# Attention beside channel mix on one core: attention steps spread over two chunks, early batches placed by load arrival, token mix as scale and add

## The chip, the cores and the metric

One core of a Trainium2 chip. The time is the device time of one execution in microseconds (us); a kernel is quoted by the median of its runs. TensorE (PE) does matmuls and transposes, VectorE (DVE), ScalarE (ACT) and GpSimd (POOL) the rest; here GpSimd mostly issues loads. "Span" is the length of one profiled execution; the timed run is 1.7 to 1.9 us longer than its span. The "granted clock" is the share of TensorE's full clock that the profile says it was given: 1.00 is full speed.

## The reference, cut to what matters

```python
# B=8 batches, H=8 heads, S=576 tokens, D=64, M=32 memory slots; model width 512, hidden 1024
a   = softmax(phi over tokens)                 # [b, h, s, m]
k_m = einsum('bhsm,bhsd->bhmd', a, k)          # v_m the same from v
x   = softmax(q @ k_m.T / 8 over m) @ v_m      # heads side by side: [B, S, 512]

x_prev = x shifted by one token (zero ahead of the first)
xk = mu_k * x + (1 - mu_k) * x_prev            # token mix for the keys
xr = mu_r * x + (1 - mu_r) * x_prev            # token mix for the gate
out = sigmoid(xr @ w_r) * (relu(xk @ w_k)**2 @ w_v)
```

The channel mix (the last line) of batch b needs the attention of batch b. The kernel writes the mix as `(x - x_prev) * (mu - 1) + x`.

## The kernel before

The channel mix runs in nine chunks of 512 tokens. A chunk has 16 slots: 8 key steps, then gates and values. After the channel-mix step of a slot the program emits the attention steps that a plan puts there. In these traces VectorE, TensorE and ScalarE run their own instructions in the order in which the program emits them (in the kernel before, TensorE stops 4.0 us for the q of batch 2 with matmuls of chunk 0 behind it). So the plan decides both what fills TensorE's time and what stands in front of what.

```python
        return [                                      # plan of a batch: (slot relative to its chunk, step)
            (-12, exp_phi),
            (-11, tr_q(0)), (-11, tr_q(1)), (-11, tr_q(2)), (-11, tr_q(3))] + kvsteps + [
            (-5, scores(0, 0)), (-4, scores(0, 1)), (-3, scores(1, 0)), (-3, scores(1, 1)),
            (-1, zsum)] + late + [
            (1, spread(0, 0)), (1, spread(0, 1)), (2, spread(1, 0)), (2, spread(1, 1)),
            (3, values(0, 0)), ...                    # cut: two values in each of slots 3 to 6
            (7, diff(0)), (8, diff(1)),
            (9, mix(0, 0)), ...                       # cut: eight mixes, to slot 14
        ]

        def mix(d4, which):
            def go():
                dst = (xk_T, xr_T)[which]
                nc.vector.scalar_tensor_tensor(
                    dst[:, d4, b * S:(b + 1) * S], in0=st["d"][:, d4, :],
                    scalar=mu1[:, which * ND + d4:which * ND + d4 + 1], in1=st["x"][:, d4, :],
                    op0=AL.mult, op1=AL.add)
            return go
```

`kvsteps` are the sums over k and v (into `kvps`, `zps`), their norm and the transpose of k (`ktps`, copied to `kmT`). PSUM, the memory in which the matmuls of this kernel leave their results, is split here into three rings of buffers that are used again and again: keys use two (`pk`), gates and values share three (`tag="pv"`), and every attention step shares three more:

```python
    kvps = psum.tile([128, 2, 2, 2 * D], F32, name="kvps", tag="at", bufs=3)   # and zps, ktps, qtps,
    ps   = psum.tile([128, SEG], F32, name="zcps", tag="at", bufs=3)           # scps, rbps, nops
    pv   = psum.tile([128, Dm], F32, name="pv", tag="pv", bufs=3)              # and pr of the gates
```

A step that asks for a fourth "at" buffer waits until one of the three has been read out by VectorE or ScalarE.

The softmax here doesn't subtract the row's maximum and nothing guards it: scores larger than these inputs give would overflow.

## Time and profile before

| | before |
|---|---|
| median at the start (3 runs) | 287.25 us (284.94 to 287.82) |
| span of the profiled run | 284.2 us |
| TensorE busy | 223.9 us |
| VectorE busy | 170.0 us |
| first key matmul | 33.3 us |
| chunks 0 and 1 | 48.2 and 32.9 us |
| chunks 2 to 5 together | 111.1 us |
| chunks 6, 7, 8 | 19.2, 17.1, 17.4 us |

A chunk is counted from its first key matmul to that of the next (the last to its last matmul). The prediction shows the lines.

### The profile page before, as it was taken

The page shows a single profiled execution, that of the slowest core. Times are in us where ns is not written, and L with a number is a line of the kernel's source. Part 1 is how long each engine was busy: PE and PEld are TensorE (multiplying, and loading weights), DVE is VectorE, ACT ScalarE, POOL GpSimd, SP SyncE. Part 2 cuts the span into 40 slices and gives each one's busy share as a digit, 9 for nine tenths or more (in the row PEclk, how much of TensorE's full clock was granted, in tenths as well). Part 3 has the DMA queues.
Part 4 walks back from the last instruction along what each step waited for, and adds up shares of the span by engine and source line. Part 5 has one row for each costly group of instructions (what it writes and reads, how often), then busy time and mean ns, then how long its engine had stood idle before and what let it go on. Part 6 is the DMA issues. An engine that isn't in the chain of part 4 may idle for free. (4 is left out here: it accounts for less than half of the span.)

```text
span 284.2 us, 4445 instructions
## 1 busy us (share of the span) xinstructions
PE 223.9 (79%) x1711; PEld 118.0 (42%) x1737; DVE 170.0 (60%) x403; ACT 105.2 (37%) x221; POOL 43.0 (15%) x60
## 2 busy tenths in 40 slices
PE   0357594698667779877987799779987999999992
PEld 0235133354323445444544454445453554444441
DVE  7325663154587487739763976497668759733411
ACT  3002351422422732462247225722661373451730
POOL 8326241143300240024002400000000000000000
PEclk9999997999956999999999999999999999999998
DMA  7999999998980399339924993012101311402124
GB/s 141 202 204 202 201 191 201 204 195 163 182 102 0 84 128 193 81 87 124 197 76 89 118 201 77 0 39 74 38 2 38 86 27 37 111 2 112 37 45 103
DMA packets 59397, 31.22 MB, mean 110 GB/s; under 512 B 18408, under 2 KB 54768, under 8 KB 59376
## 3 DMA queue, kind: packets, MB, share of 16 engines
q0 software_dynamic: 41312, 16.78, 49.2%
q1 hardware_dynamic: 18064, 14.16, 19.6%
q8 instruction: 13, 0.21, 0.3%
q14 instruction: 8, 0.07, 0.1%
HBM read 38.28 MB, written 9.44 MB: 168 GB/s over the span
## 5 line engine op out<-in xcount | busy, mean ns | idle before, releaser
L389 PE MATMUL pk<-xkT,wk 128*128 128x512 bf16 x272 | 73.5, 401 | 7.7 <-DVE xkT L323 4.9
L394 ACT ACTIVATE rl<-pk 128x512 bf16<-128x512 f32 x72 | 42.9, 595 | 77.0 <-PE pk L389 77.0
L413 PE MATMUL pv<-wv,sq 128*128 128x512 bf16 x280 | 65.2, 379 | 1.2 <-issue 1.1
L395 DVE TENSOR_TENSOR sq<-rl 128x512 bf16<-128x512 bf16 x72 | 30.2, 425 | 44.6 <-ACT rl L394 44.3
L416 DVE SCALAR_TENSOR_TENSOR o<-th,pv 128x512 f32<-128x512 f32 x36 | 24.7, 687 | 35.3 <-PE pv L413 18.9
L389 PEld LDWEIGHTS <-wk 128*128 128x128 bf16 x288 | 27.8, 102 | 38.2 <-issue 16.0
L413 PEld LDWEIGHTS <-sq 128*128 128x128 bf16 x288 | 27.6, 98 | 30.6
L405 ACT ACTIVATE th<-pr 128x512 f32<-128x512 f32 x36 | 21.4, 596 | 44.2 <-PE pr L402 33.5
L402 PE MATMUL pr<-wr,xrT 128*128 128x512 bf16 x142 | 35.2, 379 | 0.1
L243 PE MATMUL qtps<-identity,q 128*64 128x128 bf16 x320 | 14.0, 242 | 15.7 <-ACT x L303 7.6
L261 ACT ACTIVATE e<-scps 128x288 bf16<-128x288 f32 x32 | 12.3, 410 | 35.8 <-PE scps L259 35.7
L303 ACT CAST x<-nops 128x288 bf16<-128x288 f32 x64 | 22.0, 405 | 9.1 <-PE nops L301 9.0
L323 DVE SCALAR_TENSOR_TENSOR xrT<-diff,mu,x 128x576 bf16<-128x576 bf16 x32 | 24.9, 810 | 0.0
L323 DVE SCALAR_TENSOR_TENSOR xkT<-diff,mu,x 128x576 bf16<-128x576 bf16 x32 | 24.5, 813 | 0.3
L402 PEld LDWEIGHTS <-xrT 128*128 128x128 bf16 x144 | 13.8, 98 | 14.5
L83 POOL DMA_DIRECT2D q<-in_q_dram x8 | 7.2, 898 | 81.3 <-PE qtps L243 78.8
L243 PEld LDWEIGHTS <-q 128*64 128x64 bf16 x320 | 11.5, 123 | 19.0 <-issue 10.4
L259 PE MATMUL scps<-qT,kmT 128*128 128x288 bf16 x64 | 12.7, 305 | 8.0 <-DVE kmT L234 7.8
L247 DVE COPY qT<-qtps 128x576 bf16<-128x576 bf16 x32 | 13.5, 452 | 7.9 <-PE qtps L243 7.4
L200 PE MATMUL kvps<-kv,em 128*64 128x256 bf16 (+1 forms) x200 | 14.4, 272 | 4.5 <-DMA kv<-in_v_dram 2.3
L301 PE MATMUL nops<-atn,vbd 128*128 128x288 bf16 x64 | 15.3, 308 | 1.2 <-DVE atn L292 0.8
L200 PEld LDWEIGHTS <-em 128*64 128x64 bf16 x360 | 12.8, 120 | 8.4 <-issue 8.4
(58 smaller groups left out, 166.3 us busy)
## 6 DMA issues: line engine op xcount, KB each, us to landing
out_dram<-o SPq DMA_DIRECT2D x40, 128.0 KB, 2.4
phm<-in_phi_dram SPq DMA_DIRECT2D x8, 512.0 KB, 6.6
q<-in_q_dram POOLq DMA_DIRECT2D x8, 512.0 KB, 8.1
kv<-in_k_dram POOLq DMA_DIRECT2D x8, 512.0 KB, 8.2
kv<-in_v_dram POOLq DMA_DIRECT2D x8, 512.0 KB, 9.9
out_dram<-o SPq DMA_DIRECT2D x16, 256.0 KB, 2.5
wk<-in_moe_w_k_dram POOLq DMA_DIRECT2D x4, 256.0 KB, 15.3
wv<-in_moe_w_v_dram POOLq DMA_DIRECT2D x1, 1024.0 KB, 15.7
```

The lines of the kernel that those rows point to most:

```text
L200: nc.tensor.matmul(o, lhsT=lhsT, rhs=rhs, start=first, stop=j == NB, skip_group_check=True)
L243: nc.tensor.matmul(ps[i * D:(i + 1) * D, j * 128:(j + 1) * 128], lhsT=q5[:, 2 * pr + i, j, :], rhs=identity, is_transpose=True, start=True ...
L301: nc.tensor.matmul(ps, lhsT=st["vbd"][:, pr // 2, pr % 2, :], rhs=st["at"][:, pr // 2, sl], start=True, stop=True)
L303: nc.scalar.copy(st["x"][:, pr, sl], ps)
L323: nc.vector.scalar_tensor_tensor(dst[:, d4, b * S:(b + 1) * S], in0=st["d"][:, d4, :], scalar=mu1[:, which * ND + d4:which * ND + d4 + 1], ...
L389: nc.tensor.matmul(pk, lhsT=wk_sb[:, di, fi * 128:(fi + 1) * 128], rhs=xk_T[:, di, t0:t0 + CT], start=(di == 0), stop=(di == ND - 1))
L394: nc.scalar.activation(rl, pk, AF.Relu, scale=0.5 ** 0.5)
L395: nc.vector.tensor_mul(st["sq"][:, fi, :], rl, rl)
L402: nc.tensor.matmul(pr, lhsT=xr_T[:, di, t0 + ts * 128:t0 + (ts + 1) * 128], rhs=wr_sb[:, di, :], start=(di == 0), stop=(di == ND - 1))
L405: nc.scalar.activation(th, pr, AF.Tanh, scale=0.5)
L413: nc.tensor.matmul(pv, lhsT=st["sq"][:, fi, ts * 128:(ts + 1) * 128], rhs=wv_sb[:, fi, :], start=(fi == 0), stop=(fi == NF - 1))
L416: nc.vector.scalar_tensor_tensor(o, in0=st["pr"][ts], scalar=1.0, in1=pv, op0=AL.add, op1=AL.mult)
```

## The change

The intent: (1) two free slots between dependent attention steps of a batch, so that TensorE does not stop for the step just ahead, over up to two chunks; (2) batches 0 and 1 placed where their loads arrive, batch 2 squeezed into chunk 1, and a batch's phi loaded just ahead of its k, q, v; (3) the mix as a scale (`tensor_scalar`) and an add, in place of one `scalar_tensor_tensor`. The diff cut to this:

```diff
-        def mix(d4, which):
-                nc.vector.scalar_tensor_tensor(dst..., in0=d, scalar=mu1..., in1=x, op0=AL.mult, op1=AL.add)
+        def mix(which, pr, n=1):
+                dst = (xk_T, xr_T)[which][:, pr:pr + n, b * S:(b + 1) * S]
+                t = work.tile([128, 2, S], BF16, name="mu_d", tag="mu_d")[:, :n]
+                for i in range(n):
+                    o = which * ND + pr + i
+                    nc.vector.tensor_scalar_mul(t[:, i], st["d"][:, pr + i, :], mu1[:, o:o + 1])
+                nc.vector.tensor_add(dst, st["x"][:, pr:pr + n], t)
...
+    def load_batch(b):
+        load_phi(b, nc.sync if b == 0 else nc.gpsimd)     # then k, q, v; reload() calls it for b + 2
...
+        if b <= 1:
+            at = [-1] * 5 if b == 0 else [9, 11, 12, 13, 14]      # batch 1: slots of chunk 0
...
+        plan = [
+            (-16, exp_phi),
+            (-14, tr_q(0)), (-14, tr_q(1)), (-13, tr_q(2)), (-13, tr_q(3)),
+            (-8, ekv(slice(0, 2))), (-8, norm_k), (-5, tr_k), (-5, norm_v), (-5, reload),
+            (-3, scores(0, 0)), (-3, scores(0, 1)), (-2, scores(1, 0)), (-2, scores(1, 1)),
+            (1, zsum),
+            (4, spread(0, 0)), (4, spread(0, 1)), (5, spread(1, 0)), (5, spread(1, 1)),
+            (6, values(0, 0)), ...                                # two values in each of slots 6 to 9
+            (10, diff(0, 2)), (11, mix(0, 0, 2)), (11, diff(2, 2)), (12, mix(0, 2, 2)),
+            (13, mix(1, 0, 2)), (14, mix(1, 2, 2)),
+        ]
+        first = {2: 0, 3: -8}.get(b, -16)          # batches 2 and 3 squeezed into fewer slots
+        return [(15 - (15 - r) * (15 - first) // 31, s) for r, s in plan]
```

Chunk 0 also does all its gates ahead of its values, and three buffer counts of work tiles change (`rl` 4 to 3, `th` 2 to 4, `diff` 2 to 1).

More of the change, by code (lines that the diff above doesn't have):

```diff
@@ L71, with load_phi @@
     loads = {}
-    def load_phi(b):
+    def load_phi(b, eng):
         phm = ld.tile([128, H, NB, M], F32, name="phm", tag="phm")
         pht = ld.tile([NT, H, M], F32, name="pht", tag="pht")
-        nc.sync.dma_start(
+        eng.dma_start(
             out=phm.rearrange("p h j m -> p h (j m)"),
             in_=phi[b, :, 0:TAIL, :].rearrange("h (p j) m -> p h (j m)", j=NB))
-        nc.sync.dma_start(out=pht, in_=phi[b, :, TAIL:S, :].rearrange("h s m -> s h m"))
+        eng.dma_start(out=pht, in_=phi[b, :, TAIL:S, :].rearrange("h s m -> s h m"))
         loads[b] = {"phm": phm, "pht": pht}
@@ L86, in load_rows @@
         nc.gpsimd.dma_start(out=dst[:NT, :, NB, :], in_=src[:, TAIL:S, :].rearrange("h s d -> s h d"))
-    def load_kv(b):
+    def load_batch(b):
+        load_phi(b, nc.sync if b == 0 else nc.gpsimd)
         load_rows(kvs[b % 2][:, 0], k[b])
+        load_rows(qs[b % 2], q[b])
         load_rows(kvs[b % 2][:, 1], v[b])
-    def load_q(b):
-        load_rows(qs[b % 2], q[b])
     for i in range(2):
@@ L99 @@
         nc.vector.memset(kmTs[i], 0.0)
-    load_phi(0)
-    load_q(0)
-    load_kv(0)
+    load_batch(0)
     mu2 = const.tile([2 * ND, 128], F32, name="mu2")
@@ L114 @@
     nc.gpsimd.dma_start(out=wv_sb, in_=moe_w_v.rearrange("(fo fi) d -> fi fo d", fi=128))
-    load_phi(1)
-    load_rows(kvs[1][:, 0], k[1])
-    load_q(1)
-    load_rows(kvs[1][:, 1], v[1])
+    load_batch(1)
     ident_f = const.tile([2 * ND, 2 * ND], F32, name="identf")
@@ L168, in attention, with ekv @@
         st = {}
-        L = loads[b]
         kv5, q5, em, kmT = kvs[b % 2], qs[b % 2], ems[b % 2], kmTs[b % 2]
         def exp_phi():
+            L = loads[b]
             nc.scalar.activation(em[:, 0:NB].rearrange("p j h m -> p h j m"), L["phm"], AF.Exp)
             nc.scalar.activation(em[:NT, NB], L["pht"], AF.Exp)
-            if b + 2 < B:
-                load_phi(b + 2)
-        def ekv(parts, with_z):
+        def ekv(parts):
             w = parts.stop - parts.start
+            with_z = parts.start == 0
             def go():
-                if "kvps" not in st:
-                    st["kvps"] = psum.tile([128, 2, 2, 2 * D], F32, name="kvps", tag="at", bufs=3)
+                kvps = psum.tile([128, 2, w, 2 * D], F32, name="kvps", tag="at", bufs=3)
+                for i in range(w):
+                    st["kv"[parts.start + i]] = kvps[:, :, i, :]
                 if with_z:
@@ L194, in go @@
                                     rhs = kv5[:, parts, 2 * pr:2 * pr + 2, j, :]
-                                    o = st["kvps"][jj * 64:(jj + 1) * 64, c, parts, :]
+                                    o = kvps[jj * 64:(jj + 1) * 64, c]
                                 else:
@@ L198, in go @@
                                     o = st["zps"][jj * 64:(jj + 1) * 64, c:c + 1]
-                                first = j == 0 and c == 0 and (what == 1 or parts.start == 0)
-                                nc.tensor.matmul(o, lhsT=lhsT, rhs=rhs, start=first,
+                                nc.tensor.matmul(o, lhsT=lhsT, rhs=rhs, start=j == 0 and c == 0,
                                                  stop=j == NB, skip_group_check=True)
-                if parts.stop == 2 and b + 2 < B:
-                    load_kv(b + 2)
             return go
@@ L211, in norm_k @@
                 nc.vector.scalar_tensor_tensor(
-                    kbd[:, c].rearrange("p h d -> p (h d)"), in0=st["kvps"][:, c, 0, :],
+                    kbd[:, c].rearrange("p h d -> p (h d)"), in0=st["k"][:, c, :],
                     scalar=rz[:, c:c + 1], in1=maskk.rearrange("p h d -> p (h d)"),
@@ L220, in norm_v @@
                 nc.vector.scalar_tensor_tensor(
-                    vbd[:, c], in0=st["kvps"][:, c, 1:2, :].to_broadcast([128, 2, 2 * D]),
+                    vbd[:, c], in0=st["v"][:, c].unsqueeze(1).to_broadcast([128, 2, 2 * D]),
                     scalar=st["rz"][:, c:c + 1], in1=maskv.rearrange("p j h d -> p j (h d)"),
@@ L224, in norm_v, with reload @@
             st["vbd"] = vbd
+        def reload():
+            if b + 2 < B:
+                load_batch(b + 2)
         def tr_k():
@@ L247, in go @@
                 nc.vector.tensor_copy(st["qT"][:, pr, :], ps[:, 0:S])
-                if pr == NPAIR - 1 and b + 2 < B:
-                    load_q(b + 2)
             return go
@@ L304, in values, with diff @@
             return go
-        def diff(part):
+        def diff(pr, n=1):
             def go():
-                x = st["x"]
-                if part == 0:
-                    st["d"] = work.tile([128, ND, S], BF16, name="diff", tag="diff")
-                d = st["d"]
-                if part == 0:
-                    nc.vector.tensor_sub(d[:, :, 128:TAIL], x[:, :, 128:TAIL], x[:, :, 0:TAIL - 128])
-                else:
-                    nc.vector.tensor_sub(d[:, :, 1:128], x[:, :, 1:128], x[:, :, TAIL - 128:TAIL - 1])
-                    nc.vector.tensor_copy(d[:, :, 0:1], x[:, :, 0:1])
-                    nc.vector.tensor_sub(d[:, :, TAIL:S], x[:, :, TAIL:S], x[:, :, TAIL - 1:S - 1])
+                if "d" not in st:
+                    st["d"] = work.tile([128, ND, S], BF16, name="diff", tag="diff", bufs=1)
+                x, d = st["x"][:, pr:pr + n], st["d"][:, pr:pr + n]
+                nc.vector.tensor_sub(d[:, :, 128:TAIL], x[:, :, 128:TAIL], x[:, :, 0:TAIL - 128])
+                nc.vector.tensor_sub(d[:, :, 1:128], x[:, :, 1:128], x[:, :, TAIL - 128:TAIL - 1])
+                nc.vector.tensor_copy(d[:, :, 0:1], x[:, :, 0:1])
+                nc.vector.tensor_sub(d[:, :, TAIL:S], x[:, :, TAIL:S], x[:, :, TAIL - 1:S - 1])
@@ L318, in diff @@
             return go
-        def mix(d4, which):
+        def mix(which, pr, n=1):
             def go():
-                dst = (xk_T, xr_T)[which]
-                nc.vector.scalar_tensor_tensor(
-                    dst[:, d4, b * S:(b + 1) * S], in0=st["d"][:, d4, :],
-                    scalar=mu1[:, which * ND + d4:which * ND + d4 + 1], in1=st["x"][:, d4, :],
-                    op0=AL.mult, op1=AL.add)
-            return go
-        if b == 1:
-            return [
-                (6, exp_phi), (12, ekv(slice(0, 1), 1)), (12, norm_k), (13, tr_k),
-                (14, tr_q(0)), (14, tr_q(1)), (14, tr_q(2)), (14, tr_q(3)),
-                (15, scores(0, 0)), (15, scores(0, 1)), (15, scores(1, 0)), (15, scores(1, 1)),
-                (15, ekv(slice(1, 2), 0)), (15, norm_v), (15, zsum),
-                (15, spread(0, 0)), (15, spread(0, 1)), (15, spread(1, 0)), (15, spread(1, 1)),
-                (15, values(0, 0)), (15, values(0, 1)), (15, values(1, 0)), (15, values(1, 1)),
-                (15, values(2, 0)), (15, values(2, 1)), (15, values(3, 0)), (15, values(3, 1)),
-                (15, diff(0)), (15, diff(1)),
-                (15, mix(0, 0)), (15, mix(1, 0)), (15, mix(2, 0)), (15, mix(3, 0)),
-                (15, mix(0, 1)), (15, mix(1, 1)), (15, mix(2, 1)), (15, mix(3, 1)),
-            ]
@@ L344, in attention @@
-        if b == 0:
-            kvsteps = [(-10, ekv(slice(0, 1), 1)), (-10, norm_k), (-9, tr_k)]
-            late = [(-2, ekv(slice(1, 2), 0)), (-2, norm_v)]
-        else:
-            kvsteps = [(-7, ekv(slice(0, 2), 1)), (-7, norm_k), (-6, tr_k), (-6, norm_v)]
-            late = []
-        return [
-            (-12, exp_phi),
-            (-11, tr_q(0)), (-11, tr_q(1)), (-11, tr_q(2)), (-11, tr_q(3))] + kvsteps + [
-            (-5, scores(0, 0)), (-4, scores(0, 1)), (-3, scores(1, 0)), (-3, scores(1, 1)),
-            (-1, zsum)] + late + [
-            (1, spread(0, 0)), (1, spread(0, 1)), (2, spread(1, 0)), (2, spread(1, 1)),
-            (3, values(0, 0)), (3, values(0, 1)), (4, values(1, 0)), (4, values(1, 1)),
-            (5, values(2, 0)), (5, values(2, 1)), (6, values(3, 0)), (6, values(3, 1)),
-            (7, diff(0)), (8, diff(1)),
-            (9, mix(0, 0)), (9, mix(1, 0)), (10, mix(2, 0)), (10, mix(3, 0)),
-            (11, mix(0, 1)), (12, mix(1, 1)), (13, mix(2, 1)), (14, mix(3, 1)),
-        ]
+                dst = (xk_T, xr_T)[which][:, pr:pr + n, b * S:(b + 1) * S]
@@ new lines, in go @@
+                t = work.tile([128, 2, S], BF16, name="mu_d", tag="mu_d")[:, :n]
[3 more added lines that the diff above has]
+                nc.vector.tensor_add(dst, st["x"][:, pr:pr + n], t)
+            return go
+        if b <= 1:
+            at = [-1] * 5 if b == 0 else [9, 11, 12, 13, 14]
+            plan = [
+                (at[0] - 3, exp_phi), (at[0], ekv(slice(0, 1))), (at[0], norm_k), (at[0], tr_k),
+                (at[1], tr_q(0)), (at[1], tr_q(1)), (at[1], scores(0, 0)), (at[1], scores(0, 1)),
+                (at[2], tr_q(2)), (at[2], tr_q(3)), (at[2], scores(1, 0)), (at[2], scores(1, 1)),
+                (at[3], ekv(slice(1, 2))), (at[3], norm_v), (at[3], zsum), (at[3], reload),
+                (at[4], spread(0, 0)), (at[4], spread(0, 1)),
+                (at[4], spread(1, 0)), (at[4], spread(1, 1)),
+            ]
+            for pr in range(NPAIR):
+                plan += [(at[4], values(pr, 0)), (at[4], values(pr, 1)),
+                         (at[4] + b, diff(pr)), (at[4] + b, mix(0, pr))]
+            plan += [(15 * b, mix(1, pr)) for pr in range(NPAIR)]
+            return plan
@@ new lines, in attention @@
+        plan = [
+            (-16, exp_phi),
[4 more added lines that the diff above has]
+            (4, spread(0, 0)), (4, spread(0, 1)), (5, spread(1, 0)), (5, spread(1, 1)),
+            (6, values(0, 0)), (6, values(0, 1)), (7, values(1, 0)), (7, values(1, 1)),
+            (8, values(2, 0)), (8, values(2, 1)), (9, values(3, 0)), (9, values(3, 1)),
+            (10, diff(0, 2)), (11, mix(0, 0, 2)), (11, diff(2, 2)), (12, mix(0, 2, 2)),
+            (13, mix(1, 0, 2)), (14, mix(1, 2, 2)),
+        ]
@@ L391, in go @@
                                      start=(di == 0), stop=(di == ND - 1))
-                rl = work.tile([128, CT], BF16, name="rl", tag="rl", bufs=4)
+                rl = work.tile([128, CT], BF16, name="rl", tag="rl", bufs=3)
                 nc.scalar.activation(rl, pk, AF.Relu, scale=0.5 ** 0.5)
@@ L403, in go @@
                                      rhs=wr_sb[:, di, :], start=(di == 0), stop=(di == ND - 1))
-                th = work.tile([128, Dm], F32, name="th", tag="th", bufs=2)
+                th = work.tile([128, Dm], F32, name="th", tag="th", bufs=4)
                 nc.scalar.activation(th, pr, AF.Tanh, scale=0.5)
@@ L419, in value @@
             return go
+        if c == 0:
+            return [key(fi) for fi in range(NF)] + [gate(t) for t in range(4)] + [
+                value(t) for t in range(4)]
         return [key(fi) for fi in range(NF)] + [
             gate(0), gate(1), value(0), gate(2), value(1), gate(3), value(2), value(3)]
-    work_at = {}
     made = {}
@@ L431, in steps_of @@
         return made[b]
-    slots = {}
-    for b in range(B):
-        base = 16 * (b - 1)
-        for rel in range(-12, 16):
-            slots.setdefault(base + rel, []).append((b, rel))
-    last = 16 * NCH
-    for s in range(-28, last):
-        mixing = channel_mix(s // 16) if s >= 0 and s % 16 == 0 else None
-        if mixing:
-            work_at["m"] = mixing
+    for s in range(-4, 16 * NCH):
         if s >= 0:
-            work_at["m"][s % 16]()
-        for b, rel in slots.get(s, []):
+            if s % 16 == 0:
+                mixing = channel_mix(s // 16)
+            mixing[s % 16]()
+        for b in range(max(0, s // 16), min(B, s // 16 + 4)):
             for r, step in steps_of(b):
-                if r == rel:
+                if r == s - 16 * (b - 1) if b > 0 else r == s:
                     step()
```

## The prediction

> **What bounds the kernel now.** I read the page first, then the busy times cut at the starts of the nine chunks (a chunk is 512 tokens of channel mix, 16 slots), then the waits of TensorE in single chunks, the timeline of TensorE, and the issues of the GpSimd queue. The chunk starts are the first key matmul after the last value matmul of the chunk before.
>
> ```profile
> PE 223.9 (79%) x1711; PEld 118.0 (42%) x1737; DVE 170.0 (60%) x403; ACT 105.2 (37%) x221; POOL 43.0 (15%) x60
> ...
> 33.30:81.50 48.20, 35.45 (x319) 18.86 (x324) 23.56 (x58) 14.71 (x32) 13.21 (x17) 0.92 1.39 189
> 81.50:114.50 33.00, 27.17 (x200) 13.78 (x204) 23.85 (x50) 11.97 (x26) 4.71 (x6) 0.86 0.63 92
> 114.50:142.80 28.30, 23.62 (x199) 12.88 (x202) 19.42 (x44) 11.98 (x26) 4.72 (x6) 1.00 0.80 127
> 142.80:170.90 28.10, 23.65 (x199) 12.88 (x202) 19.42 (x44) 11.99 (x26) 4.71 (x6) 1.00 0.75 119
> 225.60:244.80 19.20, 18.83 (x99) 9.16 (x101) 15.37 (x31) 9.22 (x20) 0.00 (x0) 1.00 0.24 52
> 244.80:262.00 17.20, 17.15 (x79) 7.81 (x80) 6.16 (x12) 7.16 (x12) 0.00 (x0) 1.00 0.20 64
> ```
>
> The columns are stretch and length, busy PE, weight loads, DVE, ACT, POOL, granted clock, DMA share, GB/s. No engine is full over the whole span, but the stages differ. The last two chunks (17.2 us each) have no attention and no idle PE: they are the floor of a chunk. Chunks 2 to 5 take 27.1 to 28.3 us, of which PE works 23.6; chunk 0 takes 48.2 and chunk 1 33.0. So the kernel is bound by PE at the end, by PE with holes in the middle, and by something else at the start. The holes of a middle chunk (142.8 to 170.9):
>
> ```profile
> PE qtps L243 <- ACT x L303: 1.5, 1, 1.5
> PE scps L259 <- DVE kmT L234: 1.4, 1, 1.4
> PE rbps L287 <- DVE rhl L276: 0.9, 1, 0.9
> PE nops L301 <- DVE atn L292: 0.3, 1, 0.3
> ```
>
> These are attention steps that stand in the next slot, or the same one, after the step that feeds them, while DVE still works on something else. With small issue gaps they are the 28.1 - 23.6 = 4.5 us. Then the start:
>
> ```profile
> 33.30 2.77 PE L389 MATMUL pk<-xkT,wk 128*128 128x512 bf16 x4 [2.97 <-DVE xkT L323]
> 46.22 2.34 PE L243 MATMUL qtps<-identity,q 128*64 128x128 bf16 x40 [4.01 <-DMA q<-in_q_dram]
> 55.07 0.30 PE L200 MATMUL kvps<-kv,em 128*64 128x256 bf16 x2 [2.30 <-DMA kv<-in_v_dram]
> 74.76 0.54 PE L287 MATMUL rbps<-rhl,selb 112*128 112x96 bf16 x9 [1.54 <-DVE rhl L276]
> 81.54 2.77 PE L389 MATMUL pk<-xkT,wk 128*128 128x512 bf16 x4 [1.95 <-DVE xkT L323]
> 84.54 1.48 PE L389 MATMUL pk<-xkT,wk 128*128 128x512 bf16 x3 [0.22 <-issue]
> ```
>
> The reader is to see that in chunk 0 PE, which runs in program order, stops for q and v of batch 2 (46.2 and 55.1 us), although chunks 0 and 1 need nothing of batch 2. DMA moves about 200 GB/s without a break until 80 us, so these loads could not come sooner. Batch 1's attention then runs as one serial chain from 66.5 to 81.5 us, and chunk 1's first keys wait for its mixes, which come 0.73 us apart. The granted clock is 0.50 from 78 to 90 us.
>
> [...] The trace agrees for tensor_tensor: 1536 elements take 952 ns and 508 take 418, 0.52 ns an element plus about 155 ns. The scalar_tensor_tensor of the mix takes 810 ns for 576 elements, 1.14 ns an element after that constant[...]. No bf16 tensor_scalar of such size is in this trace[...]. [...] phi of batches 1 and 2 was issued from sync at 2.95 and 6.08 us, ahead of batch 0's v. [...]
>
> **The change part by part.**
>
> (1) Mixes. Before, a batch has 8 mixes of 0.81 = 6.5 us and differences of 0.95 + 0.42 + 0.17 + 0.29 = 1.8. After, per batch from the third on: [...]4 adds of 1152 at 0.6 + 0.155 = 755 ns[...]; differences in two halves of 555 + 287 + 167 + 222 = 1.23 us, 2.5. Sum 8.0 against 8.3: the DVE saves almost nothing. Batches 0 and 1 pay more[...], but each 128-row part can begin as soon as its own x is there. I see no gain in DVE busy time as such; it should be about 170 us again.
>
> (2) Start of batch 0. DMA bytes ahead of v(0) fall: before three phi, q, k and v, six loads of 0.59 MB = 3.5 MB, landed at 21.1 us (when the issue that waits for it went on). At 205 GB/s that puts the origin at 3.8 us. After, only one phi: k at 9.6, q at 12.4, v at 15.3 us. Chain from the before durations: k sums and norm to 11.3, k transpose to 12.4, q transposes, copies and scores of both halves to 18.2, v sums 19.5, zsum 20.6 (before 24.8), reciprocal chain 21.9, spread and values to 26. Diffs and mixes per part overlap values: DVE is free of atn at 24.1, four parts of 1.25 us (start to start) end at 29.1. Before, keys flowed from 35.9. Gain 6.8 us.
>
> (3) Chunk 0. Batch 2's steps leave it. Load arrival at 205 GB/s after v(0): weights 20.4, 23, 28.1; phi, k, q, v of batch 1 at 31, 34, 37, 40 us. Slots 6, 9, 11, 13 fall near 34, 37, 40 and 45 us, so no load should stop PE. PE work: 17.25 (80 matmuls) + batch 1's attention 6.4 + its back-to-back steps, which still stand in one slot: about 1 us each after the k norm and after the two q copies, 0.4 for the reciprocal, and 2.3 more for spread and values at ACT's pace (8 x 0.35 us) = 29.3 -> 58.4. Then chunk 1's first key needs the last of four mixes of batch 1, which DVE begins only after the last value's output: 0.7 + 4 x 1.25 = 5.7 -> 64.1. Before, 84.3. Gain so far 20 us.
>
> (4) Chunk 1. It holds all of batch 2 (31 slots squeezed into 16) and the first part of batch 3: PE 17.25 + 6.4 + 3.1 = 26.7; DVE about 24 from start to start. Add 1.5 for short chains and 2.5 for a cold clock after the 5.7 us hole: about 31 -> 95. Before, 114.5.
>
> (5) Chunks 2 to 5. PE work stays 23.6. Two free slots (2 us or more) cover ACT's casts and the reciprocal chain. What I expect to remain: kmT stands on DVE behind an output, two diffs and a mix, about 4.3 us after the value of slot 10, against 3.6 us of PE work, so 0.7, plus issue gaps of 0.5: 25 a chunk, 26 for chunk 2 with batch 3 still squeezed. 26 + 3 x 25 = 101 -> 196. Before 111.
>
> (6) Chunks 6, 7, 8: 20, 17.3, 17.3 -> 250.6; the tail after the last matmul was 284.2 - 279.3 = 4.9 -> span 255.5. The timed median was 287.25 against a span of 284.2; I add 2.5: **258 us**.
>
> **The rivals.** (a) Loads decide chunk 0 anyway. For it: DMA runs at 200 GB/s until 80 us, and phi now goes through GpSimd, whose 60 instructions become 74, in one row with k, q and v, eight in flight. Then chunk 0 ends where v(1) plus a chain of some 20 us puts it, and a few us late loads give 262 to 266. Against it: the bytes that chunk 0 needs end at 40 us even if my origin is 2 us off. (b) DVE becomes the bound of the middle chunks. It works 19.4 of 28 us; in 25 us that is 78%, and in the last third of a chunk diffs, mixes, outputs and kmT queue up, so scores and the next chunk's squares could wait. If the saved slots reappear as waits for kmT of 2 us, chunks 2 to 5 stay at 27: 266. Against it: PE has slots 14 to 16 to absorb it. (c) [...]a scale costs 455 ns[...], mostly hidden; +2 us. (d) All waits go: 23.8 per chunk and a warm chunk 1 give 250.
>
> **Range and chances.** The end (chunks 6 to 8 and tail) is known within 1 us. The middle is 101 with +-5, chunk 1 +-3, the start +-5; taken together +-8, a little more above than below, since rivals (a) to (c) all add: 250 to 267. To be within 2% of before, the change would have to lose 23 of its expected 29 us. Faster 0.96, same 0.03, slower 0.01.
>
> **What would show it.** Keys flowing from about 29 us; no TensorE wait for q or v in chunk 0; a hole of 4 to 6 us on xkT at the start of chunk 1 (58 to 64 us); chunks 2 to 5 at 25 us with the wait of qtps for ACT and of rbps for rhl gone and some of kmT left; chunks 7 and 8 unchanged at 17.3; [...]adds near 755. I am wrong if PE stops for loads in chunk 0, if chunks 2 to 5 stay above 27 us, or if chunk 1 grows past 35.

(1) came, with the eight scales in, to 8.0 us of VectorE a batch from the third on, and to 9.8 for each of batches 0 and 1; that VectorE's load would stay was the author's estimate from them. The 1.25 us of a part in (2) and (3) hold one such scale and are the author's estimate, and so are 29.1 and 64.1, which rest on them. The span of 255.5 and the 258 us have all these terms in. The 455 ns of rival (c) are an estimate from the two tensor_tensor figures, 0.52 ns an element plus 155.

On the clock, the trace before shows 0.50 from 47 to 49 us, after the stop of 4.01 us, and from 78 to 90; TensorE works 27.2 us in chunk 1, which holds part of that, and 23.6 us in chunk 2, at a clock of 1.00, with 200 and 199 recorded matmuls. "Eight in flight" in (a): GpSimd's first eight load issues in the trace before follow each other, and the ninth, at 11.20 us, stands 3.4 us for the first q to land. DMA moved 190 to 208 GB/s in each 10 us from 10 to 70, and 168 from 70 to 80; that batch 2's loads could not come sooner is the author's estimate from this.

## The result, and the profile after

| | before | after | predicted |
|---|---|---|---|
| median | 286.65 us (4 runs, 284.94 to 287.82) | 273.65 us (4 runs, 272.42 to 274.80) | 258 (250 to 267) |
| span | 284.2 | 272.7 | 255.5 |
| VectorE busy | 170.0 | 169.8 | about 170 |
| last key mix of batch 0 ends | 35.4 | 29.6 | 29.1 |
| last key mix of batch 1 ends | 83.7 | 67.4 | 64.1 |
| chunk 2 starts | 114.5 | 98.8 | 95 |
| chunk 2 | 28.3 | 33.2 | 26 |
| chunks 3, 4, 5 | 28.1, 27.6, 27.1 | 28.2, 26.9, 26.3 | 25, 25, 25 |
| chunks 6, 7, 8 | 19.2, 17.1, 17.4 | 19.7, 17.3, 17.4 | 20, 17.3, 17.3 |

The ratio of after to before is 0.955, with a 95% interval of 0.948 to 0.962. A ratio is the mean time of one kernel's fast runs over that of the other's fast runs of the same rounds, so it is not quite the ratio of the medians. The change gains 13 us where 29 were expected. The prediction says that keys "flow" from 29.1 and 64.1 us; its sums end there with the last of four mixes, so that event is compared here. (Its 35.9 and 84.3 for the kernel before are 0.5 and 0.6 us later than that event.)

All of the gain lies ahead of chunk 2, which starts 15.7 us earlier. Chunks 2 to 5 take 114.6 us together, 3.5 more than before, where 10 less were predicted.

First, of the kernel after, the busy times of the engines over the whole span:

```profile
PE 227.4 (83%) x1708; PEld 117.1 (43%) x1737; DVE 169.8 (62%) x491; ACT 105.3 (39%) x221; POOL 54.4 (20%) x74
```

Busy time has not fallen by more than 1 us on any engine (before: 223.9, 118.0, 170.0, 105.2, 43.0); what fell is waiting. The same by chunk (stretch and length, then busy PE, weight loads, DVE, ACT, POOL, granted clock, DMA share, GB/s):

```profile
98.80:132.00 33.20, 27.41 (x211) 14.59 (x213) 22.06 (x63) 13.51 (x30) 9.37 (x12) 0.95 1.03 143
132.00:160.20 28.20, 24.03 (x199) 12.98 (x202) 20.71 (x57) 11.84 (x26) 6.30 (x8) 1.00 0.66 108
160.20:187.10 26.90, 24.06 (x199) 12.99 (x202) 18.76 (x53) 11.85 (x26) 0.00 (x0) 1.00 0.30 62
187.10:213.40 26.30, 24.02 (x199) 12.92 (x202) 18.80 (x53) 11.85 (x26) 0.00 (x0) 1.00 0.11 41
```

TensorE works 24.0 us in each of chunks 3 to 5; the rest, 4.2, 2.8 and 2.3 us, is idle. Chunk 2 is apart: 3.4 us more work, part of it at a lower clock (a mean of 0.57 from 107 to 111 us), and 5.8 us idle. What TensorE waits for in chunk 3 of the kernel after (who waits, who ends the wait: us in total, times, longest):

```profile
PE qtps L238 <- DVE rzf L266: 1.5, 1, 1.5
PE qtps L238 <- DVE qT L242: 0.9, 1, 0.9
PE scps L252 <- DVE kmT L229: 0.7, 1, 0.7
PE zps L193 <- ACT x L296: 0.5, 1, 0.5
```

Only the third is a wait for data: scores read `kmT`. The transposes of q (`qtps`) read q and an identity; they do not read `rzf`, the reciprocal of the softmax sums, nor `qT`, which is the copy of an earlier transpose. Nor do the sums over em (`zps`) read x. Where the releaser made nothing that the waiting instruction reads, the wait is for a buffer: the releaser is the one that reads the buffer out. TensorE's timeline of the same chunk shows it (start, length, instructions, and in brackets the idle time before them with who ended it):

```profile
133.72 0.67 PE L262 MATMUL zcps<-e,selz 128*128 128x96 bf16 x12
...
135.18 0.75 PE L238 MATMUL qtps<-identity,q 128*64 128x128 bf16 x20
...
138.39 0.47 PE L238 MATMUL qtps<-identity,q 128*64 128x128 bf16 x10 [1.49 <-DVE rzf L266]
139.74 0.47 PE L238 MATMUL qtps<-identity,q 128*64 128x128 bf16 x10 [0.88 <-DVE qT L242]
```

`zcps` and two transposes (x10 each) fill the three buffers. The third transpose waits for the one of `zcps`, the fourth for that of the first transpose. VectorE's timeline says why `zcps` is read so late:

```profile
136.25 0.76 DVE L318 TENSOR_TENSOR xrT<-x,mu_d 128x1152 bf16<-128x1152 bf16 x1
136.92 0.76 DVE L386 TENSOR_TENSOR sq<-rl 128x512 bf16<-128x512 bf16 x2
137.59 0.74 DVE L266 RECIPROCAL rzf<-zcps 48x96 f32<-48x96 f32 x1
...
139.23 0.81 DVE L242 COPY qT<-qtps 128x576 bf16<-128x576 bf16 x2
```

The reciprocal stands behind the last gate mix of the previous batch and two squares. `zcps` was ready at 134.4 us and was read out at 138.3. Before the change the same ring showed as the transposes waiting for `ACT x`, a line that the prediction quoted and took for a wait on the step just ahead.

In chunk 2 of the kernel after, TensorE's largest stops are, by its timeline:

```profile
100.55 1.46 PE L380 MATMUL pk<-xkT,wk 128*128 128x512 bf16 x6 [1.19 <-DVE xkT L318]
...
105.67 0.71 PE L252 MATMUL scps<-qT,kmT 128*128 128x288 bf16 x4 [2.68 <-DVE kmT L229]
```

and VectorE ahead of that `kmT`:

```profile
98.74 0.97 DVE L317 TENSOR_SCALAR mu_d<-diff,mu 128x576 bf16<-128x576 bf16 x2
99.74 0.76 DVE L318 TENSOR_TENSOR xkT<-x,mu_d 128x1152 bf16<-128x1152 bf16 x1
...
101.74 0.65 DVE L317 TENSOR_SCALAR mu_d<-diff,mu 128x576 bf16<-128x576 bf16 x2
102.42 0.76 DVE L318 TENSOR_TENSOR xrT<-x,mu_d 128x1152 bf16<-128x1152 bf16 x1
103.09 0.95 DVE L317 TENSOR_SCALAR mu_d<-diff,mu 128x576 bf16<-128x576 bf16 x2
104.08 0.76 DVE L318 TENSOR_TENSOR xrT<-x,mu_d 128x1152 bf16<-128x1152 bf16 x1
104.75 0.75 DVE L386 TENSOR_TENSOR sq<-rl 128x512 bf16<-128x512 bf16 x2
105.42 0.48 DVE L229 COPY kmT<-ktps 128x64 bf16<-128x64 bf16 x4
```

Batch 2, squeezed into one chunk, has its mixes at the very end of chunk 1; they run on into chunk 2, and batch 3's copy to `kmT` comes after all of them in VectorE's queue. The clock then follows the stop, in windows of chunk 2 (columns as above, the clock third from the end):

```profile
98.80:107.00 8.20, 4.12 (x34) 1.98 (x34) 8.06 (x22) 3.52 (x7) 4.66 (x6) 1.00 1.32 149
107.00:111.00 4.00, 4.00 (x40) 2.13 (x35) 1.43 (x5) 1.31 (x3) 0.00 (x0) 0.57 1.50 232
111.00:132.00 21.00, 19.29 (x150) 10.48 (x148) 12.57 (x38) 8.69 (x20) 4.71 (x6) 1.00 0.83 124
```

TensorE works half of the first 8.2 us, while VectorE is full, and then 4 us at a mean clock of 0.57.

### The profile page after: what moved, and what is told of

The parts are those of the page before. It is cut to its first block, busy times and chain, and to the rows that moved or that the text cites. A ratio compares the mean times of both kernels' runs of the same rounds, so it can differ in the third digit from the quotient of the medians.

```text
span 272.7 us, 4541 instructions
## 1 busy us (share of the span) xinstructions
PE 227.4 (83%) x1708; PEld 117.1 (43%) x1737; DVE 169.8 (62%) x491; ACT 105.3 (39%) x221; POOL 54.4 (20%) x74
## 4 chain that ended last, share of the span: by engine, by line
PE 54%; DVE 23%; ACT 8%; DMA 8%; issue 5%; POOL 1%; SPq 0%; DVEq 0%; POOLq 0%
PE pk L380 17%; PE pv L404 15%; PE pr L393 8%; DMA out_dram<-o 5%; ACT x L296 4%; PE qtps L238 3%; DMA q<-in_q_dram 3%; DVE o L407 3%; DVE mu_d L317 3%; PE kvps L193 3%; PE scps L252 3%; ACT rl L385 3%; DVE sq L386 2%; DVE diff L305 2%; DVE xkT L318 2%
## 5 line engine op out<-in xcount | busy, mean ns | idle before, releaser
L380 PE MATMUL pk<-xkT,wk 128*128 128x512 bf16 x276 | 75.6, 407 | 9.8 <-DVE xkT L318 8.7
L404 PE MATMUL pv<-wv,sq 128*128 128x512 bf16 x278 | 66.7, 379 | 0.5
L380 PEld LDWEIGHTS <-wk 128*128 128x128 bf16 x288 | 27.5, 102 | 43.3 <-issue 18.5
L386 DVE TENSOR_TENSOR sq<-rl 128x512 bf16<-128x512 bf16 x72 | 29.8, 423 | 26.2 <-ACT rl L385 25.9
L317 DVE TENSOR_SCALAR mu_d<-diff,mu 128x576 bf16<-128x576 bf16 x64 | 22.0, 376 | 0.5
L254 ACT ACTIVATE e<-scps 128x288 bf16<-128x288 f32 x32 | 11.7, 408 | 23.6 <-PE scps L252 23.3
L238 PE MATMUL qtps<-identity,q 128*64 128x128 bf16 x320 | 15.0, 245 | 4.8 <-DVE qT L242 2.3
L83 POOL DMA_DIRECT2D kv<-in_k_dram x8 | 7.2, 902 | 45.0 <-PE zps L193 42.5
L285 DVE TENSOR_TENSOR atn<-e,rbps 128x288 bf16<-128x288 bf16 x32 | 12.7, 447 | 1.0 <-PE rbps L280 1.0
```

Source lines behind the costliest of these rows:

```text
L238: nc.tensor.matmul(ps[i * D:(i + 1) * D, j * 128:(j + 1) * 128], lhsT=q5[:, 2 * pr + i, j, :], rhs=identity, is_transpose=True, start=True ...
L317: nc.vector.tensor_scalar_mul(t[:, i], st["d"][:, pr + i, :], mu1[:, o:o + 1])
L380: nc.tensor.matmul(pk, lhsT=wk_sb[:, di, fi * 128:(fi + 1) * 128], rhs=xk_T[:, di, t0:t0 + CT], start=(di == 0), stop=(di == ND - 1))
L386: nc.vector.tensor_mul(st["sq"][:, fi, :], rl, rl)
L404: nc.tensor.matmul(pv, lhsT=st["sq"][:, fi, ts * 128:(ts + 1) * 128], rhs=wv_sb[:, fi, :], start=(fi == 0), stop=(fi == NF - 1))
```

## The experiments

The theories, roughly (they do not exclude each other): A, the order of work on VectorE's queue, mixes above all, holds up chunk 2 and later; B, the three PSUM buffers of the attention steps are the limit of a chunk; C, the split form of the mix ate the gain, by its extra instructions or because the scales run longer while GpSimd issues loads (0.97 us for two in place of 0.65, see r1); D, the output buffers; E, the squeeze of batch 3. Each expectation says what it means by its own. Each run was correct against the reference unless said otherwise. The chunk lengths come from one profiled execution each, counted as above (us):

| run | first key | 0 | 1 | 2 | 3 | 4 | 5 | 6 |
|---|---|---|---|---|---|---|---|---|
| before | 33.3 | 48.2 | 32.9 | 28.3 | 28.1 | 27.6 | 27.1 | 19.2 |
| after | 25.3 | 37.8 | 35.7 | 33.2 | 28.2 | 26.9 | 26.3 | 19.7 |
| r1_fused_mix | 26.1 | 38.5 | 34.5 | 32.9 | 28.0 | 27.0 | 26.4 | 19.7 |
| r2_old_middle | 23.5 | 38.9 | 39.9 | 30.7 | 30.5 | 28.7 | 27.0 | 19.2 |
| r3_middle_only | 33.7 | 50.0 | 30.5 | 26.4 | 26.4 | 26.4 | 26.4 | 19.7 |
| r4_xr_late | 24.2 | 37.7 | 35.7 | 30.6 | 30.3 | 27.9 | 27.3 | 20.7 |
| r6_at4_pv2 | 26.2 | 36.2 | 34.1 | 31.1 | 26.0 | 24.7 | 24.3 | 20.3 |
| r7_b3_full | 23.1 | 38.9 | 37.2 | 28.8 | 27.3 | 27.0 | 26.3 | 19.7 |
| r8_qT_on_act | 25.2 | 38.8 | 34.7 | 33.2 | 26.1 | 25.9 | 25.5 | 19.7 |
| r9_before_at4 | 32.1 | 48.6 | 33.1 | 26.7 | 26.7 | 26.8 | 26.4 | 19.6 |
| r10_at4_xrb2 | 24.0 | 38.4 | 33.4 | 28.8 | 26.0 | 24.9 | 24.3 | 20.2 |
| r11_at4_xrb2_qact | 25.7 | 35.7 | 33.7 | 28.2 | 24.9 | 24.4 | 24.3 | 20.2 |
| r12_old_phi | 31.6 | 37.5 | 35.6 | 31.3 | 27.5 | 26.9 | 26.3 | 19.7 |
| r13_xrb2_only | 26.1 | 38.4 | 34.6 | 30.6 | 29.4 | 27.1 | 26.3 | 19.7 |

The first key and chunk 0 move by some 1 to 3 us against each other also where their code is the same (after, r4, r7, r8, r13), so an early difference of that size is not read. Chunk 2 starts at 97.5 to 99.3 us in these five; in the three runs with four attention buffers and the new slots (r6, r10, r11) it starts at 95.1 to 96.5, so the buffers seem to cost some 2 us there as well. Chunks 3 to 5 repeat more closely.

### r1_fused_mix: the mix as one instruction again, the slots kept

```diff
-                for i in range(n):
-                    nc.vector.tensor_scalar_mul(t[:, i], st["d"][:, pr + i, :], mu1[:, o:o + 1])
-                nc.vector.tensor_add(dst, st["x"][:, pr:pr + n], t)
+                for i in range(n):
+                    nc.vector.scalar_tensor_tensor(dst[:, i], in0=st["d"][:, pr + i, :],
+                        scalar=mu1[:, o:o + 1], in1=st["x"][:, pr + i], op0=AL.mult, op1=AL.add)
```

> The changed kernel with the mix as one scalar_tensor_tensor again (8 of 0.81 us a batch in place of 8 scales and 4 adds); all else as changed. If the in-order DVE queue sets the holes of the middle chunks (theory A), about 0.5 us more DVE work per batch from start to start makes it the same to 1% slower: 273 to 277 us. If [...]the extra instructions, are what ate the gain (theory C), it is faster than the changed kernel: 268 to 271.

Measured: 274.80 us (274.58 to 276.04), ratio to before 0.963 (0.960 to 0.966), against 0.955 (0.948 to 0.962) of the change. The mixes in the kernel after and in r1, by form:

```profile
L317 DVE TENSOR_SCALAR mu_d<-diff,mu 128x576 bf16<-128x576 bf16 x64 | 22.0, 376 | 0.5
L318 DVE TENSOR_TENSOR xkT<-x,mu_d 128x1152 bf16<-128x1152 bf16 x12 | 9.1, 758 | 0.4
```

```profile
L316 DVE SCALAR_TENSOR_TENSOR xkT<-diff,mu,x 128x576 bf16<-128x576 bf16 x32 | 25.1, 815 | 0.5
```

Without the split form the kernel is 0.4% slower by the medians and 0.8% by the ratios, whose intervals overlap: the split form is worth little, and no run resolves how much. VectorE's busy time differs by 2.4 us (172.2 against 169.8) and no chunk from 2 on moves by more than 0.3. So the split form did not eat the gain either, and theory C falls, although two scales do take 0.97 and 0.95 us in place of 0.65 while GpSimd issues loads (at 98.74 and 103.09 us above; GpSimd issues from 97.11 to 101.84 and from 103.02 to 104.63).

### r2_old_middle and r3_middle_only: each half of the change alone

r2 keeps the new start and gives batches 2 to 7 the old slots (batch 2 still squeezed into chunk 1); r3 is the kernel before with the new slots, differences and mixes for batches 3 to 7 only.

```diff
 r2, in the plan of batches 2 to 7:
-            (-16, exp_phi), (-14, tr_q(0)), ...
+            (-12, exp_phi), (-11, tr_q(0)), ...      # the slots of before, two values each in 3 to 6
+            (7, diff(0, 2)), (8, diff(2, 2)), (9, mix(0, 0, 2)), (10, mix(0, 2, 2)), ...
 r3, in the kernel before:
+        if b >= 3:
+            return [ ... the plan of the change ... ]
```

> The changed kernel with the slots of before for batches 2 to 7 (batch 2 squeezed into chunk 1 so that chunk 0 stays free of it). If the two free slots were worth what I predicted (10 us in chunks 2 to 5), this loses it: 282 to 285 us. If the spread gives nothing because waits moved elsewhere (theories A and B), it is within 2 us of the changed kernel: 271 to 276.

> The kernel of before with the new slots, differences and mixes for batches 3 to 7 only; loads and batches 0 to 2 as before. If the spread is worth 10 us: 276 to 279 us. If it gives nothing (theories A and B): 284 to 288.

Measured: r2 279.97 us (278.33 to 280.71), 0.979 (0.976 to 0.982), between its two expectations; r3 279.31 us (276.96 to 281.10), 0.977 (0.971 to 0.982), just above its first. So each half is worth 6 to 7 us and they roughly add up to 13 (285.94 is the median of before beside both). In r3 the new slots settle at 26.4 us a chunk, against 27.1 to 28.3 of before: a gain of about 1.4 us, where the prediction had 2.8. Nothing early is in play there, so the limit at 26.4 belongs to the new slots with three buffers. Its waits of TensorE are those of the change's chunk 5: 0.6 for `kmT`, and 1.4 for buffers (0.6 `qT`, 0.5 `ACT x`, 0.3 `atn`).

### r4_xr_late: the gate's mixes of all batches from 2 on moved past the next chunk's first slots

```diff
-            (13, mix(1, 0, 2)), (14, mix(1, 2, 2)),
+            (21, mix(1, 0, 2)), (23, mix(1, 2, 2)),
```

> The changed kernel with the gate's mixes (2.7 us of DVE a batch) of batches 2 to 7 moved from slots 13 and 14 to slots 5 and 7 of the next chunk, where DVE has holes and the gates have not begun. Theory A (the DVE queue, overfull from slot 10 to slot 2 of the next chunk, sets the holes): chunks 2 to 5 lose 1 to 3 us each, 264 to 269 us. Theory B (the three PSUM buffers of the attention set them): no change, 272 to 275.

Measured: 276.08 us (275.68 to 276.54), 0.966 (0.965 to 0.968), outside both ranges and slower than the change if anything. Theory A falls as it was stated. Chunk 2 does fall by 2.6 us, but chunks 3 to 6 each grow by 1.0 to 2.0. Its waits of TensorE in chunk 3:

```profile
PE rbps L280 <- DVE atn L285: 1.6, 1, 1.6
PE nops L294 <- ACT x L296: 0.9, 1, 0.9
PE scps L252 <- DVE kmT L229: 0.7, 1, 0.7
PE qtps L238 <- DVE qT L242: 0.6, 1, 0.6
PE zps L193 <- ACT x L296: 0.5, 1, 0.5
```

All but the `kmT` line are buffer waits by the reading above: `atn` is what frees `rbps`, `x` what frees `nops`. The wait of the transposes for `rzf`, 1.5 us in the change, is gone, so the order on VectorE did set that one; but the later mixes now delay the readers of other buffers.

### r5_o4: four output buffers (did not run)

```diff
-                o = work.tile([128, Dm], F32, name="o", tag="o", bufs=2)
+                o = work.tile([128, Dm], F32, name="o", tag="o", bufs=4)
```

> The changed kernel with four output buffers in place of two. Theory D (the one burst of eight loads per batch at slot 11 slows the output stores, and DVE, in order, waits for an output buffer at the chunk boundary): the DVE waits on out_dram go, chunks 3 and 4 fall from 28.2 and 26.9 to about 26.4: 270 to 272 us. If the stores do not matter: 273 to 275.

It did not build, because the work tiles then needed 66.8 kB of a partition where 63.3 were left. Theory D was not tested by itself. What speaks against it is r6, which leaves the output buffers as they are and still brings chunks 4 and 5 below 25 us.

### r6_at4_pv2 and r9_before_at4: four attention buffers in PSUM, two for gates and values

```diff
-    ... tag="at", bufs=3)      # all attention tiles
+    ... tag="at", bufs=4)
-    ... tag="pv", bufs=3)      # pr and pv
+    ... tag="pv", bufs=2)
```

r6 is the change with this edit, r9 the kernel before with it. The three rings together stay at eight buffers.

> The changed kernel with four PSUM buffers for the attention and two for gate and value outputs. Theory B (three rotating buffers make the transposes wait for the reciprocal and the q copies, and the sums for ACT's casts): those waits (0.6 to 2.4 us a chunk) go, 267 to 270 us. Theory A (DVE's order): the wait moves to the next step, 272 to 276.

> The kernel of before with four PSUM buffers for the attention and two for gate and value outputs, nothing else. If the three buffers were the same limit before (its wait of the q transposes for ACT's casts, 1.5 us a chunk, is one for a buffer): chunks 2 to 5 fall from 28 to about 26.5, 279 to 282 us. If the limit came with the new slots: 285 to 288.

Measured: r6 263.15 us (261.25 to 264.72), 0.917 (0.910 to 0.925): 10.5 us below the change, more than expected. r9 282.38 us (281.90 to 284.15), 0.991 (0.987 to 0.995), just above its first range. r6 by chunk, chunks 3 to 5, and what is left of the waits in its chunk 4:

```profile
127.60:153.60 26.00, 23.85 (x200) 12.96 (x203) 20.87 (x57) 11.84 (x26) 6.31 (x8) 1.00 0.79 128
153.60:178.30 24.70, 23.72 (x200) 12.93 (x203) 18.51 (x53) 11.84 (x26) 0.00 (x0) 1.00 0.34 68
178.30:202.60 24.30, 23.39 (x199) 12.80 (x202) 18.65 (x53) 11.84 (x26) 0.00 (x0) 1.00 0.12 44
```

```profile
PE scps L252 <- DVE kmT L229: 0.6, 1, 0.6
PE pr L393 <- issue: 0.2, 1, 0.2
```

The three chunks lose 6.4 us with nearly the same TensorE work, and every buffer wait of chunks 4 and 5 is gone. In chunk 3 one is left, and it has moved on by one transpose: the third (at 132.42 us) no longer waits, the fourth waits for `rzf`:

```profile
133.93 0.47 PE L238 MATMUL qtps<-identity,q 128*64 128x128 bf16 x10 [1.04 <-DVE rzf L266]
```

That is what one buffer more should do to a wait for a buffer, and should not do to a wait for data. Two buffers for gates and values cost no visible wait there; chunks 6 to 8, which have little or no attention, grow by 0.3 to 0.6 each. The limit was in the kernel before as well, but one buffer more is worth only 0.9% there. It does not take the wait away (r9, a middle chunk):

```profile
PE scps L259 <- DVE kmT L234: 1.4, 1, 1.4
PE qtps L243 <- ACT x L303: 1.2, 1, 1.2
PE rbps L287 <- DVE rhl L276: 0.2, 1, 0.2
```

The first and the third are data waits. The second is the buffer wait of before, 1.2 us in place of 1.5. It too has moved on by one transpose: before, one (x10) ran and three (x30) waited; in r9 two ran:

```profile
147.33 0.75 PE L243 MATMUL qtps<-identity,q 128*64 128x128 bf16 x20
149.33 0.76 PE L243 MATMUL qtps<-identity,q 128*64 128x128 bf16 x20 [1.25 <-ACT x L303]
```

ScalarE reads out that buffer late, because the exp of the next batch (1.08 and 0.41 us, in the trace before at 150.40 us) stands ahead of the copy. So neither the slots (1.4 us a chunk, r3) nor the buffers (about 1.1, r9) alone give what both give together: 24.3 to 26.0 against 27.1 to 28.1.

### r7_b3_full: batch 3 with its full range of slots

```diff
-        first = {2: 0, 3: -8}.get(b, -16)
+        first = {2: 0}.get(b, -16)
```

> The changed kernel with batch 3 on its full 31 slots (its first half all in chunk 1) in place of 23. Theory E (batch 3's squeeze puts its kmT behind the backlog of batch 2's mixes at the start of chunk 2): chunk 2 falls from 33.2 to about 27, chunk 1 grows by 2 to 4: 269 to 272 us. If only the squeezed end of batch 2 loads DVE: chunk 2 stays above 30 and chunk 1 grows: 274 to 278.

Measured: 271.39 us (269.80 to 272.31), 0.947 (0.941 to 0.954), an interval that overlaps the change's. Chunk 2 falls from 33.2 to 28.8 (27 was expected) and chunk 3 by 0.9, chunk 1 grows by 1.5. Theory E holds in part: with batch 3's k transpose ahead of the boundary, the pile-up of batch 2 costs less. Part of it is only moved: TensorE works about 24.2 us in this chunk 2 (the 28.8 less 4.6 of waits), since batch 3's k transpose and scores now fall into chunk 1.

### r8_qT_on_act: the copies of the q transposes on ScalarE

```diff
-                nc.vector.tensor_copy(st["qT"][:, pr, :], ps[:, 0:S])
+                (nc.scalar.copy if b >= 2 else nc.vector.tensor_copy)(st["qT"][:, pr, :], ps[:, 0:S])
```

> The changed kernel with the copies of the transposed q (1.65 us a batch from start to start) of batches 2 to 7 on ACT in place of DVE. Theory A: DVE's queue is shorter by that just where the transposes wait for it, chunks 2 to 5 lose 0.5 to 2 us each: 268 to 271 us. If ACT's own order then delays the copies behind its squares' inputs: 273 to 276.

Measured: 269.49 us (268.88 to 270.51), 0.940 (0.935 to 0.945), in its first range. There are still three buffers, but those of the transposes are freed sooner: chunks 3 to 5 fall by 2.1, 1.0 and 0.8, and chunk 2 not at all. In chunk 3 both waits of the transposes (1.49 and 0.88) are gone. This reaches the ring from the other side, by hold time in place of count. It does not separate A from B by itself, since the same edit shortens VectorE's queue.

### r10_at4_xrb2, r11_at4_xrb2_qact and r13_xrb2_only: batch 2's gate mixes alone moved

```diff
-            (13, mix(1, 0, 2)), (14, mix(1, 2, 2)),
+            (21 if b == 2 else 13, mix(1, 0, 2)), (23 if b == 2 else 14, mix(1, 2, 2)),
```

r10 has this and r6's buffers, r11 also r8's copies, r13 this alone on the change.

> The 4/2 split of PSUM buffers, and the gate's mixes of batch 2 alone moved to slots 2 and 4 of chunk 2. Theory A for the start of chunk 2 (batch 3's kmT copies stand on DVE behind 3 us of batch 2's gate mixes, and the hole of PE brings the cold clock): the wait of 2.7 us for kmT shrinks below 1, chunk 2 falls from 31.1 to 27 to 28, 259 to 261 us. Rival (chunk 2 is long because it holds more work, or because of ACT): 262 to 264.

> As the run with the 4/2 split and batch 2's late gate mixes, and with the q copies of batches 2 to 7 on ACT. If DVE's order still sets the holes left: 0.3 to 0.6 us a chunk less, 256 to 259 us. If the PSUM split has taken those already: no change, 259 to 262.

> The changed kernel with its three attention buffers kept, and only batch 2's gate mixes moved from slots 13 and 14 to 21 and 23 (past its own squeezed range, into the first third of chunk 2). With four buffers the same move took 3.2 us (263.15 to 259.94) and 2.3 us of chunk 2. Theory 1, the two causes are independent and add up: chunk 2 falls from 33.2 to about 30.6, as where all batches' gate mixes were moved, chunks 3 to 5 stay at 28.2, 26.9 and 26.3, and the whole is 270 to 271.5 us. Theory 2, with three buffers the buffer's wait takes the place of the wait for kmT and hands the gain back in chunks 2 or 3: 273 to 274.5 us, with chunk 2 above 32 or chunk 3 above 29.

Measured: r10 259.94 us (259.17 to 261.80), 0.910 (0.908 to 0.913), in its range, with a chunk 2 of 28.8 us and a wait for `kmT` of 1.1, both a little longer than expected; its interval and that of r6 overlap, so the reading rests on the length of chunk 2. r11 259.18 us (258.85 to 259.42), 0.908 (0.907 to 0.910): no gain over r10 that the intervals separate. r13 273.30 us (272.17 to 273.81), 0.955 (0.949 to 0.960): no gain over the change that the intervals separate, though chunk 2 falls to 30.6 as theory 1 of that run said; chunk 3 grows to 29.4. Total and chunk 3 are as theory 2 had them, but not for its reason. The timeline of TensorE in r13's chunk 3, and two windows of it:

```profile
135.79 0.47 PE L238 MATMUL qtps<-identity,q 128*64 128x128 bf16 x10 [1.16 <-DVE rzf L266]
137.14 0.74 PE L238 MATMUL qtps<-identity,q 128*64 128x128 bf16 x10 [0.88 <-DVE qT L242]
```

```profile
129.70:159.10 29.40, 25.58 (x199) 13.61 (x202) 21.09 (x57) 11.92 (x26) 6.31 (x8) 0.94 0.64 104
...
137.00:139.00 2.00, 1.86 (x13) 0.93 (x13) 1.51 (x5) 0.00 (x0) 0.00 (x0) 0.50 0.11 29
```

The buffer waits are the old ones, and no longer. What is new is that here the clock falls to 0.50 after them, and TensorE works 25.58 us in this chunk in place of 24.03 for the same 199 recorded matmuls. The cold clock moved from chunk 2 to chunk 3: of the 2.6 us that chunk 2 gained, chunk 3 took back 1.2. r4's chunk 3 shows the same clock, 0.94. Why the same waits (1.49 and 0.88 us) left the clock alone in the change's chunk 3, no run tells. With four buffers one of these waits is left in chunk 3 (1.0 us for `rzf`, r6 and r10), the clock stays at 1.00 there, and the move keeps its gain: chunks 2 to 5 take 106.1 us in r6 and 104.0 in r10.

### r12_old_phi: phi issued from sync and early, as before

```diff
     def load_batch(b):
-        load_phi(b, nc.sync if b == 0 else nc.gpsimd)
...
+    load_phi(0, nc.sync)
+    load_phi(1, nc.sync)              # ahead of the weights; b + 2 in exp_phi
```

> The changed kernel with phi issued from sync as before: batch 1's at once, batch b+2's when batch b's exp is issued; k, q, v in the new order. If the bytes ahead of k, q and v of batch 0 set its start, 1.2 MB more of phi at about 200 GB/s delays the keys by 3 to 6 us: 276 to 280 us. If batch 0's own chain of steps sets it, or the early phi only moves the weights back: 272 to 275.

Measured: 276.99 us (275.82 to 277.65), 0.971 (0.967 to 0.974), 3.3 us above the change. The first key comes at 31.6 us in place of 25.3; TensorE stops at batch 0's q:

```profile
17.16 0.64 PE L241 MATMUL qtps<-identity,q 128*64 128x128 bf16 x8 [2.65 <-DMA q<-in_q_dram]
```

A part comes back later, since chunk 2 is 1.9 us shorter. Where and from which engine phi is loaded is thus a real part of the early gain; the run changes both at once, so it does not say which of them counts.

## Why the prediction was right or wrong

The direction and the places were right, the size was not: 13 us in place of 29. By its own steps:

1. **Mixes.** Right. VectorE's busy time stayed (169.8 against 170.0). The adds took 758 ns, against 755. The scales took 376 ns in the mean and two of them 0.64 to 0.65 us back to back.
2. **Start.** Right: the last mix ends at 29.6 us, not 29.1. The first difference starts 0.5 us sooner than predicted, and the four mixes follow each other by 1.47 us, not 1.25. r12 supports the cause.
3. **Chunk 0.** Right in kind: TensorE no longer stops for the loads of q and v there, and the hole on `xkT` at the start of chunk 1 is there, from 60.8 to 67.4 with single key matmuls in it. It took 2.8 us longer than predicted, 0.9 of it in that hole.
4. **Chunk 1.** Right, 31.4 us from the last mix to chunk 2 against 30.9, and by its terms: the clock after the hole is 0.50 until 72 us, as it had allowed for.
5. **Chunks 2 to 5: this step failed.** "Two free slots (2 us or more) cover ACT's casts and the reciprocal chain" named the data waits and left out the PSUM buffers. The data waits did go (`rbps` for `rhl`, up to 1.1 a chunk before), and the one wait it expected to remain, 0.7 for `kmT`, is there (0.7, 0.6 and 0.6). What it lacked in chunks 3, 4 and 5 are 3.2, 1.9 and 1.3 us above 25; the buffer waits in the three add up to 3.1 (1.49 + 0.88 + 0.50 + 0.26), 2.0 (0.9 + 0.5 + 0.3 + 0.3) and 1.4 (0.6 + 0.5 + 0.3). With a fourth buffer these chunks take 26.0, 24.7 and 24.3; of the 26.0, 1.0 is the buffer wait that one buffer more leaves. The new slots did not shorten the waits for buffers: they were 1.5 to 1.8 us a chunk before, are 1.4 with the new slots alone (r3), and more in chunks 3 and 4 of the change.
   The other missing term is chunk 2, 33.2 against 26. "26 for chunk 2 with batch 3 still squeezed" gave 1 us to the squeeze. In fact batch 2's mixes, at the end of its one chunk, run over the boundary and hold back the last `xkT` (1.2 us) and batch 3's `kmT` (2.7 us), and the clock falls after it. TensorE works 27.4 us there and 26.0 in r13, where the clock stayed at 1.00: about 1.4 us is the cold clock, by nearly the same number of recorded matmuls (211 and 210). Against r7's 24.2 us, 1.8 us are steps of batch 3 that its squeeze leaves in this chunk. Buffer waits are there too (0.7 `ktps` and 0.4 `nops`, both for `ACT x`). r10 brings the chunk to 28.8: 25.6 us of TensorE's work, and waits of 1.2 for `xkT`, 1.1 for `kmT`, 0.5 and 0.2 for ScalarE.
6. **Chunks 6 to 8 and the tail.** Right: 19.7, 17.3, 17.4 against 20, 17.3, 17.3; the tail 4.9 as predicted. The 2.5 us from span to median was 1.0 (1.7 for the profiled run itself).

The deviations of the span add up: 0.5 + 2.8 + 0.5 (steps 2 to 4) + 7.2 + 6.4 (step 5) - 0.2 (step 6) = 17.2, and the span was 272.7 against 255.5, 17.2 more. Repairing both terms of step 5 (r10) gives 259.94 us, near the 258 predicted. That the totals come so close is partly luck: r10's profiled span is 260.0 us, 4.5 above the sum's 255.5, and 2.8 of that is chunk 2.

Of the rivals, (a) did not happen. (b) came in chunk 2 only: one wait for `kmT` of 2.7 us. Elsewhere VectorE was no bound by its load, but its order set how long a PSUM buffer was held. (c), slower scales, was seen in single instructions (0.97 us for two in place of 0.65) and had no weight (r1, without the scales, is not faster: 274.80 us). None of the four named the buffers, and this is why the range was too narrow on the upper side. Of the prediction's own signs of being wrong, one came: chunks 2 and 3 stayed above 27 us (chunk 1 is 35.7 from its first key, but 31.4 as the prediction counted it).

The buffers could have been read from the profile before: the line `PE qtps L243 <- ACT x L303: 1.5` was quoted and read as a wait for the step that feeds it, and x is no operand of a q transpose. That one line was 1.5 of the 2.8 us a chunk that the prediction hoped to gain.

Left open: whether the output buffers cost anything (theory D), what sets off the clock's fall after one pair of stops (1.16 and 0.88 us, r13) and not after its twin (1.49 and 0.88, the change), and what a fifth attention buffer would do.

## What to carry to other kernels

For each wait in the profile ask first whether the releaser makes an operand of the one that waits. If not, it is a wait for a buffer, and slots between dependent steps need not cure it. A buffer more moves it on by one step, which may be enough (r6: none is left in chunks 4 and 5) or not (r9: 1.2 us in place of 1.5); an earlier read-out shortens it (r8: the 1.49 and 0.88 us are gone). When steps are spread over more slots, count for each buffer of a small ring how long it is now held and who reads it out behind what. And before work is squeezed into a shorter stretch, look at what stands behind it at the seam, in the queue of an engine that runs in program order as VectorE does here (`kmT`: 2.7 us).
